# Rearranging the opening of a spectral-filter and gated-MLP kernel: doubling copies, weight loads, bank order and eviction order

## The chip, the cores and the metric

The kernel runs on one core of one Trainium2 chip. The metric is the device time of one execution in microseconds; the median of three runs before the change is 497.5 us (496.58 to 497.59). The engines are PE (matmul), DVE (vector), ACT (scalar activation), POOL (GpSimd) and SP (which only issues DMAs here). DMAs issued by POOL run on the software queue q0 and may convert fp32 to bf16 on the way; those issued by SP run on the hardware queue q1.

## The reference

```python
# x: 8 x 3072 x 256; filt_r, filt_i: 1537 x 256; w1, w2: 256 x 1024; w_out: 1024 x 256
X = np.fft.rfft(x, axis=1)
y = np.fft.irfft(X * (filt_r + 1j * filt_i), n=3072, axis=1)
t = y.reshape(8 * 3072, 256)
out = np.maximum(t @ w1, t @ w2) @ w_out
```

All inputs and the output are fp32; the kernel computes in bf16 with fp32 accumulation.

## The kernel before, in words

**The arithmetic.** A length of 3072 is split into 96 times 32. For each batch there are four matmul stages: `f1` or `s1` (a DFT of 96 with the table C1 or CT), `s2` (a DFT of 32 with twiddles, table U), a pointwise product with the filter F (`product`), `s3` (the inverse of `s2`, tables VP and VQ), and `s4` or `s4g` (the inverse of 96, table G1 or G2). The blocks v = 0 to 5 of `s2`, `product` and `s3` each cover two of twelve window groups w. The MLP then runs per tile tt of 384 tokens: max(a, b) is computed as relu(a - b) + b, so `moe_h` multiplies with Wd = w1 - w2 and takes the relu (written to gt), and `moe_o` multiplies the relu with Wo (w_out in bf16) and y with M = w2 w_out. M is made on the chip by `prep_t` (transposes of w2b, the bf16 copy of w2) and `prep_m`.

**The opening** handles batch 0 alone and keeps its intermediate values on the chip: `s1t`, `t1` (transposes into bt), `s2`, `products`, `s3t` (which writes a transposed result into zT), `t2` (transposes of zT into zr) and `s4`. `s3t` opens with one or two filler matmuls into its bank, and so does `spin` elsewhere. From the first `moe_h` on, a plan written out by hand (`plan`, `mid`, by steps of one `moe_h` each) mixes the MLP of batch b with the spectral stages of batch b + 1 and the loads of batch b + 2 (`load_xf` into three XF buffers on SP, `fold` on POOL).

**The order on each queue is the order of the program** (`manual_schedule`); engines wait for each other by semaphores, and a tile of a pool waits for the release of the buffer that it takes over. PSUM has two pools, `ps` with six banks and `pso` with two.

**What the change touches, by queue.**

- POOL's DMAs: `load_x` (L89; a chunk of x, converted to bf16, with batch 1's chunks in four transfers of 384 KB written), `load_f` (L122; the filter, sixteen transfers), `load_wo` (L294). POOL's arithmetic: `put_fz` (L142), products of blocks 0, 2, 3, 4 (L390) from copies of PSUM that `stage_x` (L652) makes on ACT, a quarter of block 5's second product (`shared_product`, L398), `prep_wd` (L298, Wd in four quarters), `cast_w2` (L291, w2b in two halves), `table_ct`.
- SP's DMAs: `load_fn` (L138), `double_f` with an engine other than DVE (L130; rows 32 to 63 and 96 to 127 of F as copies of the rows 32 below them, from SBUF to SBUF, for window groups 8 to 12), `load_w` (L287, L288; w1 and w2 in fp32 into WS, by halves of the hidden dimension), then the writes of `f1` (L338) and `load_xf` (L94).
- DVE: table arithmetic, `t1` evictions (L575), `double_f` for window groups 0 to 8 (L128, four copies), `fix_f` (L145; one row), products (L390), two evictions of `s3t` (L595).
- ACT: sines (L191 for C1, L249 for U in two halves), evictions of tables (`put_v`, L278 and L279), `stage_x` (L652), evictions of `s3t` (L597), then those of `t2` (L613), `f1` (L335), `s4` (L464) and `moe_h` (L486).
- PE: `table_v` (L265 to L269), `s2` (L384), `s3t` (L581 fillers, L587 products), `t2` (L608), `f1` (L330), `s4` (L460), `moe_h` (L482), `prep_t` (L305), `moe_o` (L536 for Wo, L534 for M), `prep_m` (L312).

At step 8 of the plan the first `moe_o` comes up, which is the first use of Wo; `prep_t` stands at steps 7 and 8, `prep_m` at step 9, and batch 1's `f1` of chunks 4 to 15 at steps 5 to 12.

Of the kernel before, what the change touches and what calls it, by code (L numbers as in the profile page):

```python
# [15 lines left out]
D = 256  # L16
HID = 1024
NP = 96
# [9 lines left out]
def kernel(  # L28
# [43 lines left out]
    setup = ExitStack()  # L72
    init = setup.enter_context(tc.tile_pool(name="init", bufs=1))
# [50 lines left out]
    def double_f(h, g, ri, engine):  # L124
        w0, w1 = WP[h]
        o_, i_ = F[64 * g + 32:64 * g + 64, ri, w0:w1], F[64 * g:64 * g + 32, ri, w0:w1]
        if engine is V:
            V.tensor_copy(o_, i_)  # L128
        else:
            nc.sync.dma_start(out=o_, in_=i_)  # L130
# [13 lines left out]
    def fix_f():  # L144
        V.tensor_copy(F[32:33, 0, 0, 0], FZ[32:33, 0])  # L145
# [10 lines left out]

    hv = init.tile([128, 2, 1], FP32)
# [22 lines left out]
    def table_c():  # L180
# [10 lines left out]
        S.activation(C1, uc.rearrange("p k r -> p (k r)"), AF.Sin, bias=zero[0:NP], scale=TWO_PI)  # L191

# [58 lines left out]
    def table_g():  # L251
        pg = ps.tile([96, NP], FP32, tag="ps", name="pg")
        TE.matmul(pg, C1, I128[0:NP, 0:NP], start=True, stop=True)
        S.activation(G1, pg, AF.Copy)
# [27 lines left out]
    WS = zrpool.tile([128, 4, HID], FP32, tag="zr", name="WS")  # L282
    w1f, w2f = WS[:, 0:2], WS[:, 2:4]

    def load_w(h):
        js = slice(512 * h, 512 * h + 512)
        nc.sync.dma_start(out=w1f[:, :, js], in_=moe_w1.rearrange("(c p) j -> p c j", p=128)[:, :, js])  # L287
        nc.sync.dma_start(out=w2f[:, :, js], in_=moe_w2.rearrange("(c p) j -> p c j", p=128)[:, :, js])  # L288

    def cast_w2(h):  # L290
        G.tensor_copy(w2b[:, :, 512 * h:512 * h + 512], w2f[:, :, 512 * h:512 * h + 512])  # L291
# [4 lines left out]
    def prep_wd(q, engine):  # L296
        js = slice(256 * q, 256 * q + 256)
        engine.tensor_tensor(Wd[:, :, js], w1f[:, :, js], w2f[:, :, js], OP.subtract)  # L298
# [23 lines left out]

    def f1(b, c, engine):
        if c == 0:
# [3 lines left out]
        at = at_[b]  # L328
        pa = ps.tile([96, 2, D], FP32, tag="ps", name="pa")
        TE.matmul(pa, C1, xb[b, c // 2][:, 2 * (c % 2):2 * (c % 2) + 2], start=True, stop=True)  # L330
# [57 lines left out]
    def product(E, v, s, px, pool=None):  # L388
# [3 lines left out]
        return pq  # L392

    def shared_product(v, s, px, xs_, pool):
        pq = pool.tile([128, 2, 2, D], BF16, tag="pq", name="pq")
        V.tensor_tensor(pq[:, 0], px, F[:, 0, 2 * v:2 * v + 2, s], OP.mult)
        V.tensor_tensor(pq[:, 1, 0], px[:, 0], F[:, 1, 2 * v, s], OP.mult)
        G.tensor_tensor(pq[:, 1, 1], xs_[:, 1], F[:, 1, 2 * v + 1, s], OP.mult)  # L398
# [178 lines left out]
    def s3t(v, pq):  # L577
        pool, tag = (ps, "ps") if v % 2 else (pso, "po")
        pz = [pool.tile([128, 2, 2, 2, 2, NM], FP32, tag=tag, name="pt%d" % g) for g in range(2)]
        for _ in range(2 if v == 1 else 1):  # L580
            TE.matmul(pz[0].rearrange("p i s r c m -> p (i s r c m)"), W1[:, 0:128], W1, start=True, stop=True)  # L581
        for i in range(2):
            for s in range(2):
                for dc in range(2):
                    for q, tab in enumerate((VP, VQ)):
                        for g in range(2):
                            TE.matmul(pz[g][:, i, s, :, dc], pq[s][64 * g:64 * g + 64, q, i, 128 * dc:128 * dc + 128],  # L587
                                      tab[64 * g:64 * g + 64, 2 * v + i, s].rearrange("p (r m) -> p r m", r=2),
                                      start=(q == 0), stop=(q == 1))
        zv = zT.rearrange("p c m (w g) q -> p w g (c m) q", g=2)  # L590
        for g in range(2):
            o_ = zv[:, 2 * v:2 * v + 2, g]
            i_ = pz[g].rearrange("p i s r c m -> p i (c m) (s r)")
            if v >= 4 and g == 1:
                V.tensor_copy(o_, i_)  # L595
            else:
                S.activation(o_, i_, AF.Copy)  # L597

    def t2(c, engines):
# [3 lines left out]
        for k, engine in enumerate(engines):  # L603
            pr = ps.tile([96, n, D], BF16, tag="ps", name="pr")
            m0 = 4 * c + n * k
            for m in range(n):
                for dc in range(2):
                    TE.transpose(pr[:, m, 128 * dc:128 * dc + 128], zT[:, dc, m0 + m].rearrange("p u q -> p (u q)"),  # L608
# [16 lines left out]
    for g in range(2):  # L625
        for ri in range(2):
            double_f(1, g, ri, nc.sync)
    for h in range(2):
        load_w(h)
# [10 lines left out]
    zT = bpool.tile([128, 2, NM, NU, 4], BF16, tag="bt", name="zT")  # L640
    for n in range(6):
        t1(n, S if n % 2 else V)
    put_v(0, 0, table_v(0, 0))
    for g in range(2):
        for ri in range(2):
            double_f(0, g, ri, V)
# [3 lines left out]
    def stage_x(v):  # L650
        t_ = init.tile([128, 2, D], FP32, name="xs%d" % v)
# [5 lines left out]
    def products(v):  # L657
        pool = pq0 if v > 2 else pqpool
        pq = [product(V, v, 0, pxs[v][0], pool)]
        if v == 5:  # L660
            pq.append(shared_product(v, 1, pxs[v][1], xs[v], pool))
        else:
            pq.append(product(G, v, 1, xs[v], pool) if v in POOLED else product(V, v, 1, pxs[v][1], pool))
# [5 lines left out]
    put_v(0, 1, table_v(0, 1))  # L669
    pxs[2] = s2(0, 2)  # L670
    stage_x(2)
    sines_u(1)
    put_v(1, 0, table_v(1, 0))
    pxs[3] = s2(0, 3)
    stage_x(3)
    put_v(1, 1, table_v(1, 1))
    for v in (1, 0, 2):
        pqs[v] = products(v)
        if v == 0:
            load_x(1, 0, 2)  # L680
    s3t(1, pqs[1])
    pxs[4] = s2(0, 4)
    stage_x(4)
    pqs[3] = products(3)
    s3t(0, pqs[0])
    pxs[5] = s2(0, 5)
    stage_x(5)
# [4 lines left out]
    for v in (4, 5):  # L692
        s3t(v, pqs[v])
    load_x(1, 2, 2)
    load_wo()
    prep_wd(0, G)
    for c in (4, 6):
        load_x(1, c, 2)
    for q in range(1, 4):
        prep_wd(q, G)  # L700
# [3 lines left out]
    setup.close()  # L704
    apool = ctx.enter_context(tc.tile_pool(name="apool", bufs=3))
# [123 lines left out]
```

## Time and profile before

| | us |
|---|---|
| median of three runs | 497.5 |
| the profiled execution | 498.64 |
| its span, first to last instruction | 496.8 |
| first transposes of `t2` start | 35.59 |
| first `moe_h` product starts | 37.73 |
| first product with Wo starts | 44.19 |

The page's busy times over the whole span are PE 483.8 us (97%), DVE 335.4 (68%), ACT 320.4 (64%) and POOL 258.7 (52%). A share over the whole span hides the opening, where PE waits and several engines take turns; so the opening is read in windows and queue by queue. All starts are us from the first instruction. In a row of a queue the first number is the start, the second the length (for several instructions, from the first to the last end), then engine, line, operation, output<-input, shapes and count; what stands in brackets is the idle time in front of it and what ended it. "Granted clock" is the share of full speed that the throttle gave PE. A DMA's time to landing counts from the start of its issue.

### The profile page before, as it was taken

The page shows a single profiled execution, that of the slowest core. Times are in us where ns is not written, and L with a number is a line of the kernel's source. Part 1 is how long each engine was busy: PE and PEld are TensorE (multiplying, and loading weights), DVE is VectorE, ACT ScalarE, POOL GpSimd, SP SyncE. Part 2 cuts the span into 40 slices and gives each one's busy share as a digit, 9 for nine tenths or more (in the row PEclk, how much of TensorE's full clock was granted, in tenths as well). Part 3 has the DMA queues.
Part 4 walks back from the last instruction along what each step waited for, and adds up shares of the span by engine and source line. Part 5 has one row for each costly group of instructions (what it writes and reads, how often), then busy time and mean ns, then how long its engine had stood idle before and what let it go on. Part 6 is the DMA issues. An engine that isn't in the chain of part 4 may idle for free.

```text
span 496.8 us, 14137 instructions
## 1 busy us (share of the span) xinstructions
PE 483.8 (97%) x5759; PEld 353.5 (71%) x5759; DVE 335.4 (68%) x535; ACT 320.4 (64%) x667; POOL 258.7 (52%) x342
## 2 busy tenths in 40 slices
PE   7699999999999999999999999999999999999997
PEld 3457777777777777777777777776777777777775
DVE  7886788468855688467855688457873688556542
ACT  5777478667775677576866668665766656464442
POOL 8694868318466594528646295536842212222220
PEclk9879999999999999999999999999999999999999
DMA  8989988996789867896789977897776834531112
GB/s 128 161 242 224 259 269 260 284 234 190 204 266 221 216 210 223 249 225 174 231 257 227 183 244 211 257 215 168 227 231 175 181 104 129 157 120 66 64 64 86
DMA packets 76626, 97.30 MB, mean 196 GB/s; under 512 B 7985, under 2 KB 54354, under 8 KB 75186
## 3 DMA queue, kind: packets, MB, share of 16 engines
q1 hardware_dynamic: 63218, 66.71, 52.1%
q0 software_dynamic: 13200, 29.60, 21.4%
q8 instruction: 45, 0.74, 0.7%
q14 instruction: 19, 0.16, 0.1%
q10 hardware_dynamic: 144, 0.09, 0.1%
HBM read 53.87 MB, written 47.19 MB: 203 GB/s over the span
## 4 chain that ended last, share of the span: by engine, by line
PE 92%; DMA 3%; ACT 2%; POOL 1%; issue 1%; DVE 0%; SPq 0%; POOLq 0%
PE po L536 34%; PE ph L482 33%; PE po L534 8%; PE pz L408 5%; PE pc L443 3%; PE px L384 2%; PE pa L355 2%; DMA xb<-in_x_dram 2%; DMA zr<-zd 1%; PE pt L587 1%; DMA zd<-zt 1%; PE pr L608 1%; POOL xb L89 1%; PE pt L581 1%; PE pa L330 1%
## 5 line engine op out<-in xcount | busy, mean ns | idle before, releaser
L486 ACT ACTIVATE gt<-ph 128x384 bf16<-128x384 f32 x357 | 175.7, 496 | 138.8 <-PE ph L482 136.2
L536 PE MATMUL po<-Wo,gt 128*128 128x256 bf16 x1528 | 262.7, 273 | 1.2 <-issue 1.2
L536 PEld LDWEIGHTS <-gt 128*128 128x128 bf16 x1528 | 144.7, 98 | 68.1 <-issue 13.5
L495 POOL DMA_DIRECT2D out_dram<-ot x186 | 103.1, 558 | 154.7 <-DVE ot L547 138.7
L390 DVE TENSOR_TENSOR pq<-px,F 128x1024 bf16<-128x1024 f32 x91 | 106.9, 1218 | 25.7 <-PE px L384 25.4
L484 DVE TENSOR_SCALAR gt<-ph 128x384 bf16<-128x384 f32 x155 | 83.6, 551 | 53.5 <-PE ph L482 47.1
L482 PEld LDWEIGHTS <-Wd 128*128 128x128 bf16 x1024 | 99.6, 98 | 13.7 <-issue 0.3
L104 POOL TENSOR_TENSOR xb<-XF 128x512 bf16<-128x512 f32 x48 | 61.3, 1277 | 66.9 <-DMA XF<-in_x_dram 31.7
L547 DVE TENSOR_SCALAR ot<-po 128x512 f32<-128x512 f32 x83 | 57.0, 686 | 35.0 <-PE po L536 33.1
L105 POOL TENSOR_TENSOR xb<-XF 128x512 bf16<-128x512 f32 x48 | 61.1, 1274 | 0.0
L359 ACT ACTIVATE at<-pa 128x512 bf16<-128x512 f32 x96 | 51.8, 611 | 3.4 <-PE pa L355 3.3
L412 ACT ACTIVATE zt<-pz 128x512 bf16<-128x512 f32 x84 | 45.6, 594 | 5.7 <-PE pz L408 1.9
L448 ACT ACTIVATE ce<-pc 128x384 f32<-128x384 f32 x56 | 23.7, 490 | 6.7 <-PE pc L443 6.0
L408 PE MATMUL pz<-pq,VP 64*64 64x256 bf16 x336 | 22.2, 281 | 0.0
L384 PE MATMUL px<-bt,U 64*64 64x256 bf16 x384 | 20.4, 283 | 1.2 <-ACT VQ L279 0.7
L408 PE MATMUL pz<-pq,VQ 64*64 64x256 bf16 x336 | 21.1, 269 | 0.0
L408 PEld LDWEIGHTS <-VP 64*64 64x64 bf16 x336 | 10.0, 105 | 13.3 <-issue 12.7
L355 PE MATMUL pa<-xb,CT 64*64 64x512 bf16 x192 | 18.0, 377 | 0.0
L443 PEld LDWEIGHTS <-zr 48*128 48x128 bf16 x896 | 13.1, 93 | 4.8 <-issue 4.4
L443 PE MATMUL pc<-G,zr 48*128 48x48 bf16 x896 | 15.4, 180 | 0.3 <-DMA zr<-zd 0.3
L384 PEld LDWEIGHTS <-U 64*64 64x64 bf16 x384 | 10.6, 109 | 3.9 <-issue 3.6
L618 PE MATMUL pd<-W 128*128 128x512 bf16 x28 | 9.2, 437 | 1.5 <-DVE zero L150 1.5
(383 smaller groups left out, 632.1 us busy)
## 6 DMA issues: line engine op xcount, KB each, us to landing
out_dram<-ot POOLq DMA_DIRECT2D x186, 128.0 KB, 3.8
XF<-in_x_dram SPq DMA_DIRECT2D x96, 192.0 KB
ad<-at SPq DMA_DIRECT2D x56, 192.0 KB
zd<-zt SPq DMA_DIRECT2D x42, 256.0 KB
zr<-zd SPq DMA_DIRECT2D x56, 192.0 KB
bt<-ad SPq DMA_DIRECT2D x13, 768.0 KB
WS<-in_moe_w_dram SPq DMA_DIRECT2D x4, 512.0 KB
xb<-in_x_dram POOLq DMA_DIRECT2D x8, 192.0 KB, 5.6
```

Source lines behind the costliest of these rows:

```text
L104: G.tensor_tensor(t_[:, 0], f[:, 0], f[:, 1], OP.add)
L105: G.tensor_tensor(t_[:, 1], f[:, 0], f[:, 1], OP.subtract)
L359: S.activation(at[:, m0:m0 + 2], pa[g], AF.Copy)
L390: E.tensor_tensor(pq, px.rearrange("p (o i) d -> p o i d", o=1).to_broadcast([128, 2, 2, D]), F[:, :, 2 * v:2 * v + 2, s], OP.mult)
L408: TE.matmul(pz[g][64 * s:64 * s + 64, i], tab[64 * g:64 * g + 64, 2 * v + i, s], pq[s][64 * g:64 * g + 64, q, i], start=(q == 0), stop=(q ...
L412: S.activation(zt[:, :, g], pz[g], AF.Copy)
L482: TE.matmul(ph, Wd[:, dc, 128 * j:128 * j + 128], y_[:, dc], start=(dc == 0), stop=(dc == 1))
L484: V.tensor_scalar(gt[tt][:, j], ph, 0.0, None, OP.max)
L486: S.activation(gt[tt][:, j], ph, AF.Relu)
L495: E.dma_start(out=dst, in_=ot[tt // 2][:, 3 * (tt % 2) + c])
L536: TE.matmul(p_, g_[:, n - 2, blk], Wo[:, n - 2], start=(e == 0), stop=(e == 9))
L547: V.tensor_scalar(ot[tt // 2][:, e - 1:e + 1], po[q // 2 % 2], SCALE, None, OP.mult)
```

## The change

The whole change lies in the opening, apart from two numbers in batch 2's load plan.

- The doubling of window groups 4 to 8 for g = 1 goes to SP's DMAs, ahead of those of groups 8 to 12; DVE keeps groups 0 to 8 for g = 0 and 0 to 4 for g = 1. `fix_f` goes to POOL.
- The first half of w1 and w2 is loaded in pieces of 256 columns (four DMAs in place of two); the second half goes into a buffer of a new pool (`whpool`), which `stage_x(3)` uses before, and is issued after `products(3)`.
- Batch 1's first x load comes after `s2(0, 4)` in place of after block 0's products; the other three and `load_wo` stand between the quarters of `prep_wd`.
- `sines_u(1)` and `table_v(1, 0)` come before `s2`; `put_v(1, 0)` follows `put_v(0, 1)`.
- Block 5's second product is done on DVE in full, with no copy by `stage_x(5)`.
- `s3t` alternates its banks over the order 1, 0, 2, 3, 4, 5; it writes PSUM with the 32 m in eights of four, zT is laid out accordingly, and the last call's eviction is cut so that its first eighth comes first. A second sine table CP holds C1's columns in the order that zT now has, for `table_g`.
- `f1` is split into its matmul (`f1_in`) and its eviction (`f1_out`); between `s3t` and the first `moe_h` four fillers (`fill`, in a `pso` bank) take the place of two `spin`s, and `f1_out` of chunks 2 and 3 moves to steps 1 and 2.
- `opool` is allocated ahead of `apool` and `zpool`. In batch 2's plan the fourth XF load moves from step 12 to 14, its fold from 20 to 23, and the next fold from 24 to 25.

```diff
-    def double_f(h, g, ri, engine):
-        w0, w1 = WP[h]
+    def double_f(w0, w1, g, ri, engine):
...
-        V.tensor_copy(F[32:33, 0, 0, 0], FZ[32:33, 0])
+        G.tensor_copy(F[32:33, 0, 0, 0], FZ[32:33, 0])
...
+        S.activation(CP.rearrange("p (g w c) -> p g w c", g=2, c=4),
+                     uc.rearrange("p (w g s) r -> p g w (s r)", g=2, s=2), AF.Sin, bias=zero[0:NP], scale=TWO_PI)
...
-        TE.matmul(pg, C1, I128[0:NP, 0:NP], start=True, stop=True)
+        TE.matmul(pg, CP, I128[0:NP, 0:NP], start=True, stop=True)
...
+    def load_w(h, cuts):
+        wh[h] = whpool.tile([128, 2, 2, 512], FP32, tag="wh", name="wh") if h else WS
+        for j0, j1 in cuts:
+            for k, w in enumerate((moe_w1, moe_w2)):
+                src = w.rearrange("(c p) j -> p c j", p=128)[:, :, 512 * h + j0:512 * h + j1]
+                nc.sync.dma_start(out=wh[h][:, k, :, j0:j1], in_=src)
...
+    def f1_in(b, c):
+        pas[c] = ps.tile([96, 2, D], FP32, tag="ps", name="pa")
+        TE.matmul(pas[c], C1, xb[b, c // 2][:, 2 * (c % 2):2 * (c % 2) + 2], start=True, stop=True)
...
     def s3t(v, pq):
-        pool, tag = (ps, "ps") if v % 2 else (pso, "po")
-        pz = [pool.tile([128, 2, 2, 2, 2, NM], FP32, tag=tag, name="pt%d" % g) for g in range(2)]
+        pool, tag = (ps, "ps") if v in (0, 3, 5) else (pso, "po")
+        pz = [pool.tile([128, 8, 2, 2, 2, 2, 4], FP32, tag=tag, name="pt%d" % g) for g in range(2)]
...
+                            TE.matmul(pz[g][:, :, i, s, :, dc].rearrange("p o r m -> p r o m"),
+                                      pq[s][64 * g:64 * g + 64, q, i, 128 * dc:128 * dc + 128],
+                                      tab[64 * g:64 * g + 64, 2 * v + i, s].rearrange("p (r o m) -> p r o m", r=2, m=4),
                                       start=(q == 0), stop=(q == 1))
...
+        for o0, o1 in ((0, 1), (1, 8)) if v == 5 else ((0, 8),):
+            for g in range(2):
+                o_ = zT[:, o0:o1, :, :, g, 2 * v:2 * v + 2].rearrange("p o c m w q -> p o (c m) (w q)")
+                i_ = pz[g][:, o0:o1].rearrange("p o i s r c m -> p o (c m) (i s r)")
...
-    for g in range(2):
-        for ri in range(2):
-            double_f(1, g, ri, nc.sync)
-    for h in range(2):
-        load_w(h)
+    for w0, w1 in ((4, 8), (8, 12)):
+        for g in range(w0 == 4, 2):
+            for ri in range(2):
+                double_f(w0, w1, g, ri, nc.sync)
+    load_w(0, ((0, 256), (256, 512)))
...
+    sines_u(1)
     for n in range(6):
         t1(n, S if n % 2 else V)
     put_v(0, 0, table_v(0, 0))
+    pv1 = table_v(1, 0)
     for g in range(2):
         for ri in range(2):
-            double_f(0, g, ri, V)
+            double_f(0, 4 if g else 8, g, ri, V)
...
-        if v == 5:
-            pq.append(shared_product(v, 1, pxs[v][1], xs[v], pool))
-        else:
-            pq.append(product(G, v, 1, xs[v], pool) if v in POOLED else product(V, v, 1, pxs[v][1], pool))
+        pq.append(product(G, v, 1, xs[v], pool) if v in POOLED else product(V, v, 1, pxs[v][1], pool))
...
     for v in (1, 0, 2):
         pqs[v] = products(v)
-        if v == 0:
-            load_x(1, 0, 2)
     s3t(1, pqs[1])
     pxs[4] = s2(0, 4)
+    load_x(1, 0, 2)
+    pqs[3] = products(3)
+    load_w(1, ((0, 512),))
     stage_x(4)
-    pqs[3] = products(3)
     s3t(0, pqs[0])
     pxs[5] = s2(0, 5)
-    stage_x(5)
...
+    prep_wd(0, G)
     load_x(1, 2, 2)
+    prep_wd(1, G)
     load_wo()
-    prep_wd(0, G)
-    for c in (4, 6):
-        load_x(1, c, 2)
-    for q in range(1, 4):
-        prep_wd(q, G)
+    prep_wd(2, G)
+    load_x(1, 4, 2)
+    prep_wd(3, G)
+    load_x(1, 6, 2)
...
-    f1(1, 0, S)
-    spin(1)
+    f1_in(1, 0)
+    fill(1)
     t2(0, (V, S))
-    f1(1, 1, V)
-    spin(1)
+    f1_in(1, 1)
+    f1_in(1, 2)
+    fill(1)
     s4(0)
-    f1(1, 2, S)
-    f1(1, 3, V)
+    f1_in(1, 3)
+    f1_out(1, 0, S)
+    f1_out(1, 1, V)
+    fill(2)
...
+    plan(0, 1, f1_out, 1, 2, S)
+    plan(0, 2, f1_out, 1, 3, V)
...
-            (8, 8, 10, 12, 17, 20, 24, 28), (10, 13, 16, 20, 24, 27, 30, 33))
+            (8, 8, 10, 14, 17, 20, 24, 28), (10, 13, 16, 23, 25, 27, 30, 33))
```

## The prediction

> **What bounds the kernel now.** I read the page first, then busy time in short windows, then the queues of PE, POOL, DVE, ACT and SP over the first 60 us, then the DMA queues and landings. In ten-microsecond windows PE is 10.00 of 10.00 from 40 us to 320 us: behind the opening nothing but PE's own work sets the time, so an edit of the opening is worth the time by which PE's unbroken stretch moves, and no more. Windows (length, busy time with count of PE, PEld, DVE, ACT, POOL, granted clock, DMA share, GB/s):
>
> ```profile
> 20.50:21.00 0.50, 0.50 (x47) 0.40 (x26) 0.47 (x2) 0.28 (x2) 0.50 (x2) 1.00 0.85 77
> 22.50:23.00 0.50, 0.00 (x0) 0.00 (x0) 0.50 (x1) 0.50 (x2) 0.00 (x0) 0.50 0.26 66
> 31.00:31.50 0.50, 0.50 (x11) 0.25 (x12) 0.50 (x1) 0.50 (x2) 0.50 (x1) 0.50 1.02 373
> 31.50:32.00 0.50, 0.50 (x31) 0.45 (x25) 0.50 (x2) 0.16 (x1) 0.50 (x1) 0.97 1.12 320
> 50.00:60.00 10.00, 10.00 (x94) 7.83 (x92) 7.06 (x13) 4.25 (x9) 8.51 (x9) 1.00 0.93 261
> ```
>
> The reader sees PE idle at 22.5, its clock at half from about 21.2 to 31.5, then full. Now the queues (start, length, instruction, idle before):
>
> ```profile
> 18.49 4.76 DVE L128 COPY F<-F 32x4096 bf16<-32x4096 bf16 x4
> 23.76 8.13 DVE L390 TENSOR_TENSOR pq<-px,F 128x1024 bf16<-128x1024 f32 x7 [0.19 <-DVE F L145]
> ...
> 26.07 6.30 POOL L390 TENSOR_TENSOR pq<-xs,F 128x1024 bf16<-128x1024 f32 x3
> 32.95 0.56 POOL L89 DMA_DIRECT2D xb<-in_x_dram  x1
> 33.51 0.93 POOL L294 DMA_DIRECT2D Wo<-in_moe_w_out_dram  x1
> 36.72 3.74 POOL L298 TENSOR_TENSOR Wd<-WS 128x512 bf16<-128x512 f32 x3
> 40.40 2.01 POOL L291 CAST w2b<-WS 128x1024 bf16<-128x1024 f32 x2
> ```
>
> ```profile
> 35.59 0.62 PE L608 MATMUL pr<-I,zT 128*96 128x128 bf16 x8 [0.34 <-DVE zT L595]
> 37.73 0.89 PE L482 MATMUL ph<-y__998,Wd 128*128 128x384 bf16 x4
> 43.74 0.61 PE L305 MATMUL pt<-I,w2b 128*128 128x128 bf16 x8
> 44.19 0.60 PE L536 MATMUL po<-Wo,gt 128*128 128x256 bf16 x4
> ```
>
> The opening ends with the transposes at 35.59; the first product with Wd runs at 37.73. Then the landing of Wo, and q0 while it moves (38 to 40 us; packets, MB, share of 16 engines):
>
> ```profile
> DMA to landing us min/median/max: 10.6/10.6/10.6
> ...
> q0 software_dynamic: 481, 0.28, 113.5%
> ```
>
> Wo is issued at 33.51 and lands at 33.51 + 10.6 = **44.11**; PE first uses it at **44.19**. That 0.08 us is the fact on which this forecast turns.
>
> **The change part by part.** All is compared with the profiled execution: 498.64 us, span 496.8 and 1.84 around it, 1.14 above the median of 497.5.
>
> *DVE.* Four copies take 4.76, 1.19 each. Of window groups 4 to 8 with g = 1 two half copies go to DMA: saved 2 x 0.6 = 1.19. The fix of one row (L145, 0.28 plus the 0.19 behind it) goes to POOL: saved 0.48. Products start at 18.49 + 3.6 = 22.1 instead of 23.76. There are now eight full ones of 8.13/7 = 1.16 (block 5's second one is no longer shared, 1.16 for 0.68 + 0.41): done at 31.4, before 32.8.
>
> *POOL.* Its filter issues end at 22.22, as before. The row fix costs between DVE's 0.28 and POOL's own cast at L142, 0.54; I take 0.5, nearer the POOL row. Then products 0, 2, the x issue (0.56, now behind product 2), products 3, 4 at 2.1 each: 22.7, 24.8, 26.9, 27.5, 29.6, 31.7; before, product 4 ended at 32.37. The shared piece (0.66) is gone. The fix waits for DVE's first copy (19.7), which is over by then. Batch 1's first x, issued at 26.9, lands 6.2 later (its landing before) at 33.1; PE's f1_in, queued ahead of the transposes, asks for it at 33.8. Then Wd quarters of 1.25 and issues in the new order: quarter 0 to 32.95, x issue to 33.5, quarter 1 to 34.75, Wo issued 34.75 to 35.7, quarter 2 to 36.95, x to 37.5, quarter 3 to 38.7, x to 39.25, casts to 40.25 and 41.25, before 41.4 and 42.4. So POOL is about 1.1 ahead, but Wo is issued 1.25 later than before.
>
> *ACT.* The extra sine of 96x96 costs 0.38 (row of L191) where ACT sits idle 1.77 at 4.3 us. The second half of U (0.93) moves from 22.97 into the 1.34 that ACT idles before 16.43. VP and VQ of the second half are then done at about 24.7, before 26.94, with one xs copy (0.60) saved. Without that idle time the sine would cost its 0.93.
>
> *PE.* The first s3t starts behind VQ's last eviction and the two products of block 1 (22.1 + 2 x 1.16 = 24.4): its two fillers at 24.8 instead of 26.0. At half clock a call is 0.54 filler + 0.97, s2 is 0.6: s3t(1) ends 26.8, s3t(0) 28.8, s3t(2) 30.9. The bank wait before s3t(2) (about 0.6, at 30.1 to 30.73, for ACT's eviction) goes, because the banks alternate. What is late next is ACT's two evictions a call, 1.09, which free s3t(4)'s bank at about 32.0; s3t(4) and (5) then end near 33.8 (before 34.7). The last eviction (0.69 on DVE) is split, so that the transposes wait for an eighth of it; a small DVE cast costs 0.28 (L145): they start at 34.15 instead of 35.59. **Gain here 1.45.** First Wd product at 36.3, first use of Wo at 42.75. The four fillers (0.22 each, before two) and the held banks lie in the time until y is evicted; without that cover 0.44.
>
> *Not shown by the trace.* Matmuls that write PSUM in runs of four: between nothing and twice the 0.57 of a call's 32, that is 0 to 3.4 over six calls; every 64-column row of L587 runs at the column rate, so I take 0. Evictions read with a stride already at L562 and L564 (0.55 and 0.43 for 384) and cost no more than contiguous ones at L484 and L486 (0.55, 0.49): 0.
>
> *SP and DMA.* Two more doubling transfers of 128 KB go ahead of the weights. Those on record took from about 20.8 (issue) to 24.6 for the first two. Their source rows land at 18.5 and 20.2, so they land at about 22.5 and 24; needed by POOL's product 2 at 24.8: hidden by 0.8. The first half of the weights goes in rows of 1 KB instead of 2 KB. From 33 to 34 us q1 moved 0.38 MB in 197 packets at 100.3%: 81 ns for 2 KB; in rows of 512 B (62 to 64 us) 1181 packets at 102.7% of 2 us: 28 ns. So 1 KB lies between 41 and 56 ns, 0 to 1.0 us for 1024 packets over 16 engines; I take 0.3. The second half waits for POOL's product 3 (29.6), whose staged input shares its buffer; nothing else is queued on SP until 36. By bytes both halves end near 34.5 to 35, as before (34.7). Batch 1's x then lands within 0.4 of before, and Wo behind it on the same queue, which is full (104 to 114% from 36 to 42): **Wo lands at 43.7, between 43.1 and 44.8**.
>
> The Trainium skill ("DMA: Bandwidth & Descriptors", Specifications) puts the smallest transfer for line rate at 512 B, by which the 1 KB rows would cost 0 and Wo land 0.3 earlier; the rows above disagree, 28 ns for 512 B being 1.4 times the per-byte time of 2 KB.
>
> *The later x load* (step 12 to 14) issues its two transfers behind batch 1's read-back; PE is 10.00 of 10 there: 0, and if that cover fails, a SP issue of 0.4.
>
> **Sum.** PE would be at Wo's first use at 42.75 but waits until 43.7, so it stands 0.45 before its old 44.19: span 496.35, execution 498.2, median **497.05**. The other 1.0 of the opening's gain turns into a wait.
>
> **Rivals.**
> *The whole gain passes.* Wo lands by 42.75: for it, the x load runs when the weights are done, and shares from 34.5 to 36 were only about 0.7; against it, Wo's own packets filled more than four microseconds at over 110%. 497.5 - 1.45 = 496.05. A clock that returns to full at 28.0 belongs here: PE is busy from 24.8 instead of idling at 25, and s3t(2), (3) at full rate would bring up to 0.4 more, 495.65. The Trainium skill ("TensorE: Matmul & The Clock Gate", Part 1) has the gate decide in free-running windows of about 3.4 us; the half-clock stretch of 10.3 us agrees, and that rule would put the earlier return at 28.
>
> *Slower: POOL becomes the bound.* Quarter 0 now stands before x and quarter 1 before Wo. If the doubled rows land late, product 2, product 3, the second half of the weights, x and Wo slip together. Between x's issue (32.95) and its first packets (about 34.3) lie 1.4 us, so Wo, issued at 34.75, could move from 36.2, while x ends at about 36.8: from 0.6 of slip on it is paid one for one. Rows 2.5 later than I have them (26.5) slip POOL 1.7: Wo at 44.8 by that, and 0.5 more where x(1,0), also late, holds PE: 45.3, **498.6**. For it: the first two such transfers took 3.8 us from issue; against it, the 0.8 in hand.
>
> *The opening does not shorten*: POOL's product 4 ends at 32.4 as before (issues end later under the added traffic), s3t(5) near 34.7, only the split helps, and Wo lands as now: 497.4.
>
> **How the numbers follow.** Forecast 0.42 (its own range 496.2 to 498.0), whole gain 0.31, POOL bound 0.18, no shortening 0.09. A measurement here tells about 0.2%, 1.0 us. Of the forecast's 0.42 some 0.12 lies beyond 1.0 faster and 0.01 beyond 1.0 slower; with the rivals: faster 0.31 + 0.12 = 0.43, slower 0.18 + 0.01 + 0.01 = 0.20, same 0.37. The range runs from the whole gain with the early clock, 495.6, to a little past the POOL case, 498.9; it leaves out the strided writes at their upper bound.
>
> **What would show it.** Right: transposes L608's counterpart near 34.2, first Wd product near 36.3, then PE idle 0.5 to 1.5 just before the first product with Wo, released by its DMA. Wrong: no idle there (whole gain), or POOL's product 2 waiting for a DMA on F, or transposes not earlier than 35.

## The result and the profile after

| | before | after |
|---|---|---|
| median, us | 497.54 | 500.82 |
| ratio, 95% interval | | 1.0064 [1.0043, 1.0084] |
| profiled execution, its span, us | 498.64, 496.8 | 501.47, 499.7 |
| first transposes of `t2` start | 35.59 | 33.87 |
| first product with Wd starts | 37.73 | 36.09 |
| first product with Wo starts | 44.19 | 48.77 |

One of the changed kernel's six executions took 1249.35 us; the median contains it and the ratio doesn't. By the ratio the change makes the kernel 3.2 us slower; the forecast was 497.05, 0.45 faster. Measured once more on another chip, beside other runs, the ratio was 1.0047 [1.0035, 1.0059].

The queue of PE after the change (start, length, instruction, idle time in front and its releaser):

```profile
33.87 0.62 PE L615 MATMUL pr<-I,zT 128*96 128x128 bf16 x8
...
36.09 0.86 PE L488 MATMUL ph<-y__1003,Wd 128*128 128x384 bf16 x4
...
41.14 0.82 PE L488 MATMUL ph<-y__1003,Wd 128*128 128x384 bf16 x2 [3.09 <-POOL Wd L303]
...
48.77 0.60 PE L542 MATMUL po<-Wo,gt 128*128 128x256 bf16 x4
```

The opening arrives 1.64 us earlier at the first product with Wd, and the third quarter of Wd isn't there. The same stretch in windows, first of the kernel after, then of the kernel before (length, busy time of PE, PEld, DVE, ACT and POOL with counts, granted clock, DMA share, GB/s):

```profile
36.09:38.05 1.96, 1.96 (x17) 1.15 (x15) 1.81 (x4) 1.37 (x3) 1.42 (x2) 1.00 1.09 231
38.05:41.14 3.09, 0.01 (x1) 0.00 (x1) 1.16 (x3) 0.49 (x1) 1.31 (x2) 0.90 0.90 156
41.14:48.77 7.63, 7.63 (x54) 5.38 (x55) 3.83 (x7) 4.06 (x7) 4.89 (x8) 0.59 1.10 207
```

```profile
37.73:44.19 6.46, 6.46 (x72) 4.75 (x71) 5.94 (x12) 5.22 (x10) 5.35 (x8) 1.00 1.15 201
```

PE does the same work in both: 1.96 + 7.63 x 0.59 = 6.46 us of full clock, as before. So the 4.58 us by which the first product with Wo is later divide as: 1.64 gained, **3.09 of wait for Wd, and 3.13 because the clock was at half from the end of that wait on** (from 40.5 to 47.4; 7.63 us for 4.50 us of work). The span grows by 2.9 only. Of the 1.68 between, 1.27 is idle time of PE behind 50 us, of which this execution has less than the one before:

```profile
50.00:490.00 440.00, 439.77 (x5068) 325.57 (x5066) 296.42 (x454) 285.12 (x596) 220.49 (x282) 1.00 0.74 199
```

```profile
50.00:490.00 440.00, 438.50 (x5058) 324.55 (x5056) 295.65 (x452) 284.28 (x595) 221.40 (x282) 1.00 0.73 198
```

The first line is after, the second before: 0.23 us of idle PE against 1.50 (the largest piece before: 1.23 at 336.35, for which the profile shows no releaser). This idle time differs between executions, of one kernel too: it is 0.70 in a second profile of the changed kernel, and over all the profiles below it lies between 0 (`e14_half_before`) and 3.20 (`e6_both_order`). So one profile tells what the opening does, and the executions of a run together tell the time.

Why Wd is late is on POOL and SP after the change:

```profile
33.59 1.27 POOL L303 TENSOR_TENSOR Wd<-WS 128x512 bf16<-128x512 f32 x1 [1.79 <-DMA WS<-in_moe_w_dram]
34.80 0.56 POOL L90 DMA_DIRECT2D xb<-in_x_dram  x1
35.37 1.28 POOL L303 TENSOR_TENSOR Wd<-WS 128x512 bf16<-128x512 f32 x1
36.59 0.92 POOL L299 DMA_DIRECT2D Wo<-in_moe_w_out_dram  x1
39.83 1.26 POOL L303 TENSOR_TENSOR Wd<-wh 128x512 bf16<-128x512 f32 x1 [2.32 <-DMA wh<-in_moe_w_dram]
```

```profile
18.71 7.27 SPq L130 DMA_DIRECT2D F<-F  x6
26.03 3.62 SPq L293 DMA_DIRECT2D WS<-in_moe_w_dram  x4
29.76 1.46 SPq L293 DMA_DIRECT2D wh<-in_moe_w_dram  x2
```

and in the chain of waits that ended last (start, length, what):

```profile
21.10 4.32 DMA F<-in_filt_i_dram
25.42 0.02 SPq L130
...
29.76 0.42 SPq L293
30.18 0.04 issue
30.22 9.53 DMA wh<-in_moe_w_dram
39.75 0.07 issue
39.83 1.27 POOL Wd L303
41.10 0.05 issue
41.14 0.82 PE ph L488 x2
```

Two things are to be seen. POOL waits twice for weights, 1.79 and 2.32 us; x and Wo stand behind the first wait, and Wo is issued at 36.59 (33.51 before). And the second half of the weights, issued at 29.76, needs 9.53 us and lands at 39.75. What it shares the DMA engines with is seen in the queues from 29 to 30 us (packets, MB, share of 16 engines), after and then before:

```profile
q0 software_dynamic: 34, 0.14, 83.6%
q1 hardware_dynamic: 8, 0.01, 2.1%
```

```profile
q0 software_dynamic: 38, 0.16, 78.3%
q1 hardware_dynamic: 34, 0.07, 19.8%
```

While batch 1's x, issued at 27.01 on POOL's queue, moves, the weights on SP's queue all but stop (0.01 MB in each of the two microseconds 29 to 31; before, beside the same x, 0.07 and 0.16). The stretch from 25 to 30 us shows the sum of it, after and then before:

```profile
25.00:30.00 5.00, 4.05 (x118) 2.67 (x121) 3.83 (x4) 2.95 (x7) 4.99 (x4) 0.81 0.69 145
```

```profile
25.00:30.00 5.00, 4.79 (x127) 2.75 (x126) 5.00 (x5) 3.33 (x8) 4.99 (x4) 0.50 0.75 204
```

145 GB/s against 204 over 5 us is 0.3 MB that the changed kernel still has to move when the DMA engines are full (share 1.02 from 30 to 35).

### The profile page after: what moved, and what is told of

It reads as the page before. It is cut to its first block, busy times and chain, and to the rows that moved or that the text cites. A ratio compares the mean times of both kernels' runs of the same rounds, so it can differ in the third digit from the quotient of the medians.

```text
span 499.7 us, 14150 instructions
## 1 busy us (share of the span) xinstructions
PE 485.5 (97%) x5757; PEld 355.3 (71%) x5761; DVE 334.5 (67%) x534; ACT 320.8 (64%) x668; POOL 257.4 (52%) x342
## 4 chain that ended last, share of the span: by engine, by line
PE 91%; DMA 4%; POOL 2%; SPq 1%; issue 1%; DVE 0%; POOLq 0%
PE po L542 35%; PE ph L488 33%; PE po L540 8%; PE pz L414 5%; PE pc L449 3%; PE pa L368 2%; PE px L397 2%; DMA wh<-in_moe_w_dram 2%; DMA xb<-in_x_dram 2%; POOL F L123 1%; DMA F<-in_filt_i_dram 1%; SPq L293 1%; POOL xb L90 1%; PE pa L336 1%; PE pr L615 1%
## 5 line engine op out<-in xcount | busy, mean ns | idle before, releaser
L403 DVE TENSOR_TENSOR pq<-px,F 128x1024 bf16<-128x1024 f32 x92 | 108.1, 1218 | 26.8 <-PE px L397 25.4
```

What stands on the lines that cost most here:

```text
L403: E.tensor_tensor(pq, px.rearrange("p (o i) d -> p o i d", o=1).to_broadcast([128, 2, 2, D]), F[:, :, 2 * v:2 * v + 2, s], OP.mult)
```

## The experiments

**Theory:** the gain of the opening is real and is lost to landings of weights, x and Wo, because these were made later, or no earlier, while PE needs them earlier. **Rivals:** batch 2's plan, the additional doubling transfers, POOL's order or the 1 KB rows by itself. Each group of runs has its own runs of the kernel before on its chip (medians 497.6 to 498.2); a difference between groups counts for less than one within a group. All ratios are against the kernel before.

### One part of the change undone

`e1_early`: all weights issued together; block 3's staged input gets a buffer of its own, so that the second half need not wait for it.

```diff
     load_w(0, ((0, 256), (256, 512)))
+    load_w(1, ((0, 512),))
...
     pqs[3] = products(3)
-    load_w(1, ((0, 512),))
```

> The changed kernel, but the second half of w1 and w2 is issued on SP right behind the first (two transfers of 512 KB), into a buffer that block 3's staged input no longer shares. Theory L (the second half comes late because its issue waits for POOL's product 3 at 29.7 and then shares the engines with x): it lands before 36.5, POOL does not wait for it, PE's 3.1 us wait for Wd and the half clock behind it are gone, PE reaches the first product with Wo at about 43 to 44.5 instead of 48.8, and the time is 496.0 to 497.5. Rival R (the rows of 1 KB in the first half let x take the engines, so that both halves come late): the second half still lands after 38, PE still waits 1.5 us or more for Wd, and the time stays at 499 to 501.

Measured 1.0031 [1.0014, 1.0049]. PE in its trace, from the third quarter on:

```profile
39.67 0.50 PE L488 MATMUL ph<-y__1003,Wd 128*128 128x384 bf16 x2 [1.76 <-POOL Wd L303]
...
41.13 0.42 PE L336 MATMUL pa<-xb,C 96*96 96x512 bf16 x1 [0.29 <-DMA xb<-in_x_dram]
...
42.99 0.62 PE L310 MATMUL pt<-I,w2b 128*128 128x128 bf16 x8 [0.48 <-POOL w2b L296]
...
45.55 0.60 PE L542 MATMUL po<-Wo,gt 128*128 128x256 bf16 x4
```

The wait for Wd is 1.76 instead of 3.09, the clock stays full, and the first product with Wo is at 45.55 instead of 48.77. In its place stand a wait for x and one for w2b, whose casts come last on POOL, behind its own waits for weights (1.39 and 1.23): the wait removed uncovers the next. The second half landed just after 38 (quarter 2 starts at 38.36), and with the wait and the time (499.39) that is what rival R expected, not theory L: the late issue isn't the cost by itself.

`e2_halves`: the first half in rows of 2 KB, the second half still late. `e3_both`: the old loading, both halves in rows of 2 KB, issued together (the diff is that of `e2_halves`; `e3_both` has the one of `e1_early` as well).

```diff
-    load_w(0, ((0, 256), (256, 512)))
+    load_w(0, ((0, 512),))
```

> The changed kernel, but the first half of w1 and w2 in two transfers of 512 KB with rows of 2 KB, in place of four with rows of 1 KB; the second half is as changed, behind product 3. Theory L: the issue of the second half stays at 29.7 and its landing moves by less than 1.5 us from 39.75; PE still waits 2 us or more for Wd, time 499 to 501. Rival R: the first half is through before x takes the engines, the second lands before 37, PE waits less than 1 us, time below 498.

> The changed kernel with the old weight loading: four transfers of 512 KB, rows of 2 KB, one behind the other, no shared buffer. Both theories: no wait for Wd. By the prediction's own forecast (Wo lands at 43.7 whatever the opening gains) PE waits at the first product with Wo until about 43.7 and the time is 496.5 to 497.5; if the opening's gain passes whole, the first product with Wo runs at 42.6 and the time is 495.7 to 496.3.

Measured 1.0037 [1.0014, 1.0061] and 1.0035 [1.0017, 1.0053]. `e2_halves` is about as theory L had it (waits of 1.80 and 0.42 for Wd). `e3_both` misses what both theories expected, no wait for Wd: PE waits 0.41, 0.52 and 1.41 us for it and 0.65 for x, and the first product with Wo is at 46.21. With whole rows quarter 0 starts at 34.62 in both (33.59 in the changed kernel, 33.21 in `e1_early`): the pieces do bring the first quarter 1.0 to 1.4 us earlier. On the time `e1_early` and `e3_both`, on one chip, do not differ (499.39 and 499.5), so the row size, rival R's cause, is no cost that shows here.

`e5_order`: POOL's old order, the rest as changed. `e6_both_order`: the same with the old weight loading.

```diff
-    prep_wd(0, G)
     load_x(1, 2, 2)
-    prep_wd(1, G)
     load_wo()
-    prep_wd(2, G)
-    load_x(1, 4, 2)
-    prep_wd(3, G)
-    load_x(1, 6, 2)
+    prep_wd(0, G)
+    for c in (4, 6):
+        load_x(1, c, 2)
+    for q in range(1, 4):
+        prep_wd(q, G)
```

> The changed kernel with POOL's old order behind the products: x, Wo, Wd's quarter 0, two x, quarters 1 to 3. Theory O (POOL waits for the first half of the weights ahead of the x and Wo issues, and these and the casts come late): Wo is issued near 32.5 instead of 36.6 and no longer stands behind a wait, but the second half of the weights, issued at 29.7, now shares the engines with x and Wo, lands after 40, and PE waits for Wd until 41 to 43: time 499.5 to 502. If the order were all there is to it, the first product with Wo comes before 45 and the time is below 498.

> The changed kernel with the old weight loading (as the third experiment) and with POOL's old order too. Theory O: Wo is issued near 32.5 and lands at 43 to 44.5, the first product with Wo comes at 43 to 44.8, time 496.3 to 497.7; that would be the forecast's own case, the gain of the opening turned into a wait for Wo. Rival D (the doubling transfers and the later first x load make the weights late whatever the order is): PE waits 1 us or more for Wd, the first product with Wo comes at 45.5 or later, time 498.5 to 500.

Measured 1.0073 [1.0047, 1.01] and 1.0045 [1.0028, 1.0061]. In `e5_order` Wo is issued at 31.98, but PE waits 3.97 us for the third quarter (41.34 on POOL, which waits 4.88 for the weights): x and Wo now move ahead of them. So POOL's new order alone is not the cost. In `e6_both_order` PE waits 1.02 for Wd and the first product with Wo is at 44.35, as before the change and as theory O had it; the time (500.29) is not. The profiled execution idles 3.2 us behind 50 us, 1.22 of it waiting for a read-back of zr at 100.06; whether the other executions lose their time there too isn't known.

`e9_plan_back`: batch 2's old load plan.

```diff
-            (8, 8, 10, 14, 17, 20, 24, 28), (10, 13, 16, 23, 25, 27, 30, 33))
+            (8, 8, 10, 12, 17, 20, 24, 28), (10, 13, 16, 20, 24, 27, 30, 33))
```

> The changed kernel with batch 2's old load plan (fourth XF load at step 12, folds at 20 and 24). Theory P (the later load keeps SP busy until 73 in place of 65, so batch 1's zd writes, its zr reads and batch 2's bt read come late, which PE meets only if it is early): here PE is 4.6 us late at the first product with Wo anyway, so the move back gains at most 0.7: 499.8 to 501.5. If the plan were the larger part of the loss, the time falls below 499.3.

Measured 1.0021 [1.0001, 1.0042], lower than the changed kernel, on another chip, and at 499.59 just under what was expected. Its trace still has the waits for Wd (1.44 and 0.41) and a first product with Wo at 46.72; nothing behind 60 us accounts for a gain by the plan. `e11_plan_alone` and `e18_early_plan` below bear on it.

### One part of the change alone, on the kernel before

`e4_gate` and `e8_gate_alone` put the late second half into the kernel before, the latter with `opool` allocated first (the last line of the diff), `e7_order_alone` POOL's new order (the diff of `e5_order` reversed), `e11_plan_alone` the new plan (the diff of `e9_plan_back` reversed).

```diff
-    for h in range(2):
-        load_w(h)
+    load_w(0)
...
     pqs[3] = products(3)
+    load_w(1)
...
+    opool = ctx.enter_context(tc.tile_pool(name="opool", bufs=2))
```

> The kernel before, with one part of the change alone: the second half of w1 and w2 goes into a buffer that block 3's staged input uses first, and is issued behind block 3's products (two transfers of 512 KB); the first half stays in two transfers with rows of 2 KB. Theory L: the issue moves from 26.3 to about 30.3, the half lands at 37.5 to 40, POOL waits for it before Wd's third quarter, PE waits 0.5 to 3 us, and the time is 498 to 501. Rival R: with rows of 2 KB the second half lands before 37 and the time stays within 0.5 us of before.

> The kernel before with POOL's new order alone (quarter 0, x, quarter 1, Wo, quarter 2, x, quarter 3, x). Theory O: quarter 0 waits for its weights until 33.5 to 34.5, x is issued near 35.3 instead of 33.0 and Wo near 37 instead of 33.5, Wo lands at 45 to 47 and PE waits for it (or for x of chunk 4) 1 to 3 us: time +1 to +3 over before. If the order is free, because the queue is full anyway, as the prediction had it: within 0.5 of before.

> The kernel before with the late second half alone (as the fourth experiment), and with the output pool allocated ahead of the pool of f1's evictions, so that no eviction waits for the weights' buffer. Theory L: the second half lands at 37.5 to 40, Wd's third quarter and with it the third of the first tile's products waits up to 2 us: time +0.5 to +2.5 over before. Rival O (the late half is harmless while x and Wo are issued early): within 0.5 of before.

> The kernel before with the new load plan of batch 2 alone. Theory P: SP's loads of XF behind batch 1's bt read hold the first zd write until 71 to 74 instead of 66.4, PE waits for zr or bt 0.5 to 3 us in all between 95 and 170, time 0.7 to 3 us over before. If the plan is free: within 0.4 of before.

Measured: `e4_gate` 1.017 [1.0145, 1.0194], `e8_gate_alone` 1.0006 [0.9988, 1.0024], `e7_order_alone` 1.0015 [0.9994, 1.0035], `e11_plan_alone` 0.9996 [0.998, 1.0011]. `e4_gate` measures something else: the weights' new buffer lies where eviction buffers come later, and ACT's evictions wait for it (PE waits 7.37 us at 45.56). It shows why the change moves `opool` to the front, which `e8_gate_alone` does too. There the second half is issued at 30.43, yet the third quarter does not wait, and the first product with Wo is at 44.50: theory L missed again. In `e7_order_alone` Wo is issued at 36.67, and PE waits 0.30 for it and 0.70 for x, the least that theory O expected; the time doesn't show it. None of the three parts costs the kernel before anything that shows in the time. That each costs something under an opening that needs the data earlier isn't shown.

### The opening alone

`e10_opening_only` is the changed kernel with the old weight loading, POOL order and plan together; `e12_x_early` also issues batch 1's first x where it was:

```diff
     for v in (1, 0, 2):
         pqs[v] = products(v)
+        if v == 0:
+            load_x(1, 0, 2)
     s3t(1, pqs[1])
     pxs[4] = s2(0, 4)
-    load_x(1, 0, 2)
```

> The changed kernel with three parts undone: the old weight loading, POOL's old order and batch 2's old load plan (the sixth experiment with the old plan). Theory P: the first zd write is issued near 66 again instead of 73, PE's waits for zr and bt near 100 and 115 are gone, and the time falls from 500.3 to 496.8 to 498.0. If the plan is free, it stays at 499.8 to 500.8.

> The tenth experiment with batch 1's first x back behind block 0's products. Theory X (the later x load stops the weights for 2 to 3 us while it runs, 27 to 30, and comes late for f1): PE's waits for x near 34 (0.4) and for Wd's third quarter near 39.6 (1.0) shrink by 0.5 or more in sum, the first product with Wo comes at 43.3 to 44.2, time 0.2 to 1.0 below the tenth. If x's place is free: within 0.3 of the tenth.

Measured 1.0022 [0.9994, 1.0051] and 1.0007 [0.9989, 1.0026]: no gain in either, and no loss that shows. DVE in the profiled execution of `e12_x_early`, at 501.26 one of its slowest (the median is 498.77), shows what an early x can do:

```profile
31.98 1.23 DVE L403 TENSOR_TENSOR pq<-px,F 128x1024 bf16<-128x1024 f32 x1 [3.81 <-DMA F<-F]
```

With x issued at 25.04 the doubled rows of groups 8 to 12, now behind two more transfers, come 3.81 us late for block 4's product; from 26 to 29 us SP's queue moves nothing. In the changed kernel x goes 2 us later, DVE waits 1.17 for the same rows, and the weights pay. The doubling, x and the weights want the same three microseconds. That this is why the typical execution gains nothing is argued, not shown.

`e15_double_dve` takes the two transfers back to DVE; `e16_double_dve_early` does so on top of `e1_early`.

```diff
-    for w0, w1 in ((4, 8), (8, 12)):
-        for g in range(w0 == 4, 2):
-            for ri in range(2):
-                double_f(w0, w1, g, ri, nc.sync)
+    for g in range(2):
+        for ri in range(2):
+            double_f(8, 12, g, ri, nc.sync)
...
-            double_f(0, 4 if g else 8, g, ri, V)
+            double_f(0, 8, g, ri, V)
```

> The changed kernel with the doubling as before: four transfers on SP for window groups 8 to 12, all of groups 0 to 8 by DVE. Theory (late second half of the weights and POOL's order are the cost): first half of the weights is issued 1 us earlier (25.0) and quarter 0 waits less (under 1.0 us, 1.79 with six transfers), products start 1.2 later, the second half still waits for product 3 and lands near 39 to 40: PE waits 2 to 3 for Wd's third quarter, ratio 1.004 to 1.007. Rival (the doubling by DMA ahead of the weights is the cost): ratio 1.002 or less, wait for Wd under 1.

> The run before it with the second half of the weights issued right behind the first as well (own buffer), so that all weights are issued about 25.0 to 29, as in the kernel before. Theory: the weights land as before (bulk by 35.5), third quarter waits under 0.5, what is left is POOL's order (Wo issued near 36, lands near 44.8): ratio 1.000 to 1.002, under the 1.003 of the same run with six transfers. Rival (the doubling by DMA costs nothing, the weights would be as late without it): ratio 1.003 or more, quarter 0 waits 1.4 as with six transfers.

Measured 1.005 [1.003, 1.007] and 1.0035 [1.0017, 1.0053]. The first has the time and the wait that the theory expected (PE waits 2.79 for Wd in the profiled execution, at 504.14 its slowest; the median is 500.52), although the weights were issued no earlier there (27.30). The second misses it and has the rival's time: no wait for Wd is left, but the transposes start only at 36.96, DVE's four copies having ended at 24.5, and the first product with Wo at 46.07. So the two transfers are not the cost by themselves. How much of the opening's gain hangs on them isn't settled: without them the transposes start at 36.96 in the second and at 34.75 in the first (35.59 before the change).

### The weights' bytes taken away

`e13_half_old_order` is `e5_order` without the load of the second half; what is worked out from it takes the first half's data, with the same instructions. `e14_half_before` does so to the kernel before.

```diff
-        wh[h] = whpool.tile([128, 2, 2, 512], FP32, tag="wh", name="wh") if h else WS
+        wh[h] = WS
...
-    load_w(1, ((0, 512),))
+    wh[1] = WS
```

> The changed kernel with only the first half of the MoE weights loaded (the second half of the difference Wd and of w2 is worked out from the first half's data; 1 MB less moves in the opening) and POOL's old order of x, Wo and quarters. Theory (the opening's gain is real and is lost only to landings of weights, x and Wo): no wait for Wd above 0.3 us, first product with Wo between 42.4 and 43.4 us (it was 44.19 before and 48.77 in the changed kernel), clock full behind 40, median 0.8 to 1.5 us under the kernel before (ratio 0.997 to 0.9985). Rival (the gain is lost elsewhere: batch 2's plan, the read-backs of zr and bt, the clock): first Wo as early, yet the ratio is 1.000 or more, with idle time of PE behind 60 us.

> The control: the kernel before with only the first half of the weights loaded, its quarters worked out from that half. Theory: it never waited for weights, so the lack of 1 MB moves only Wo and x, which landed at their use: first Wo 43.8 to 44.2, ratio 0.999 to 1.0005. Rival (the relief of the DMA engines itself is worth the time, whichever opening stands ahead of it): ratio 0.998 or less, as much as the run with the changed opening gains.

Measured 0.9982 [0.9964, 1.0001] and 1.0001 [0.9985, 1.0017]. Against `e5_order` (1.0073) one thing differs, the load of 1 MB, and it is worth 0.9% (on different chips); the first product with Wo is at 45.27 where it was at 48.89. The kernel before gains nothing from the same relief. This is the run that carries the theory: **the changed opening is slower because of the second half of the weights, and that half costs only the changed opening.** Leaving it out takes away its bytes and the waits for its landing together; the two aren't told apart. The trace is less neat than expected:

```profile
35.33 0.62 PE L615 MATMUL pr<-I,zT 128*96 128x128 bf16 x8
...
39.31 0.82 PE L488 MATMUL ph<-y__1000,Wd 128*128 128x384 bf16 x4 [0.44 <-POOL Wd L303]
...
40.53 0.50 PE L488 MATMUL ph<-y__1000,Wd 128*128 128x384 bf16 x2 [0.39 <-POOL Wd L303]
...
45.27 0.60 PE L542 MATMUL po<-Wo,gt 128*128 128x256 bf16 x4
```

In this execution the doubling occupied SP until 27.0, the opening was 1.5 us later than in the other trace, and even the first half alone came late; for the first product with Wo 42.4 to 43.4 was expected. What the second half costs is read from the twelve executions against those of `e5_order`. That the opening is faster than before without it isn't shown: the interval just includes 1 and overlaps that of `e14_half_before`, on the same chip.

### The remaining question: the plan

`e17_after_again` is the changed kernel once more; `e18_early_plan`, on the same chip, is `e1_early` with `e9_plan_back`.

> The changed kernel itself once more, beside the next run on the same chip, since the runs so far stand on different chips and the distance of the changed kernel from the run with batch 2's old plan (0.4%) is larger than any idle time behind 60 us shows. Theory (the loss is in the opening, 3 us): ratio 1.004 to 1.008, first product with Wo between 46.5 and 49 us. Rival (the first measurement was high): ratio 1.002 to 1.004.

> The changed kernel with the second half of the weights issued right behind the first and batch 2's old load plan, POOL's new order and six doubling transfers kept. Theory (only the opening counts, the plan is worth nothing): as the run with the early second half alone, ratio 1.002 to 1.0045. Rival (the plan costs 0.2 to 0.4% of its own): ratio 0.999 to 1.001.

Measured 1.0047 [1.0035, 1.0059] and 1.0047 [1.0035, 1.0059]: both edits together gain nothing on this chip. With `e11_plan_alone` that speaks against the plan, as the theory had it, but the earlier weights show no gain here either, slightly over what was expected. The profiled execution of `e17_after_again` waits 1.40 and 0.26 us for Wd and 0.47 for w2b with the clock full, and its first product with Wo is at 46.37: the loss in the opening is 2.2 to 4.6 us, by execution. In `e18_early_plan` PE has no wait for Wd at all, and the chain of waits says what took its place:

```profile
26.39 6.77 DMA WS<-in_moe_w_dram
33.15 0.02 issue
33.18 0.02 POOLq L303
33.20 0.09 issue
33.29 1.21 POOL Wd L303
34.50 7.02 DMA xb<-in_x_dram
41.52 0.04 issue
41.56 0.42 PE pa L336
```

```profile
41.56 0.42 PE L336 MATMUL pa<-xb,C 96*96 96x512 bf16 x1 [1.71 <-DMA xb<-in_x_dram]
```

POOL waits for the first half of the weights, only then issues x, x needs 7.02 us, and PE waits 1.71 for x instead of Wd. This is the part that POOL's new order plays in this execution: x behind a wait for weights.

No version ran faster than the kernel before in a way the runs can tell; the one that leaves 1 MB out comes nearest to it.

## Why the prediction was wrong

**Right:** that PE is all but unbroken behind the opening (439.77 of 440 us busy; 436.80 in `e6_both_order`), that the opening would gain about 1.45 (transposes 33.87 for a forecast 34.15, first product with Wd 36.09 for 36.3), that the gain could turn into a wait for data, ACT's times (second VQ half done at 24.5, forecast 24.7), nothing for strided PSUM writes (a row of `s3t` takes 0.20 as before) and nothing for batch 2's plan (0.9996 alone). The clock came back to full at 26.9 instead of 31.5, as the first rival had it (it put it at 28.0).

**Partly luck.** The path to the transposes was not the forecast's. DVE's products ended at 32.86, where the forecast had 31.4 and the kernel before 32.81: a wait of 1.17 for doubled rows took most of what DVE had saved. The earlier full clock, which the forecast left to a rival, worked the other way, and the two misses offset each other; no run separates them.

**Its signs.** The idle time of 0.5 to 1.5 us in front of the first product with Wo didn't come: PE runs into it without a wait. (The sum's 0.45 is 0.49 by its own 44.19 and 43.7; nothing hangs on it.)

**The step that failed** is in "SP and DMA": "By bytes both halves end near 34.5 to 35, as before (34.7)". The first half landed at 33.5 and the second at 39.75. Three terms were missing from it:
- Issue. The weights are issued at 26.03 (25.07 before), the first half in four issues of 3.62 us in all. The chain above shows what holds SP's queue: the last doubling transfer (L130) waits for the filter's last piece, which lands at 25.42. SP waits 2.0 us for such pieces, 0.7 before. The number of doubling transfers isn't it: with four instead of six the weights were issued at 27.30 (`e15_double_dve`) and 26.89 (`e16_double_dve_early`). Why the piece landed later isn't shown.
- Company. In the kernel before q1 moved 0.07 to 0.34 MB a microsecond from 27 to 32, with batch 1's x beside it from 28 on; the forecast took the weights to land as there. Beside the same x they now get 0.01 a microsecond from 29 to 31, and beside the next x, from 37 to 39, the second half's tail gets 0.04 and 0.05.
- Order. The second half is issued at 29.76, last of all; POOL's wait of 2.32 us for it holds quarter 2, and behind it x, quarter 3 and x. A late issue alone need not cost that: in `e8_gate_alone` it comes at 30.43, and POOL doesn't wait.

**What hung on it.** POOL's row without waits (quarter 0 at 31.7, Wo issued at 34.75) became 33.59 and 36.59, and Wo landed near 45.4 for a forecast 43.1 to 44.8. That no longer mattered: PE asked for the third quarter of Wd at 38.05, 3.09 us ahead of it. The forecast looked for the wait at Wo because Wo was the one landing on the edge (44.11 for 44.19); it gave no due time to Wd's quarters, which before had been ready at every use.

**Doubled rows.** "Hidden by 0.8" held here for POOL's product 2, which did not wait, but not in `e1_early` (0.56) and `e18_early_plan` (0.80). The rows of groups 8 to 12, two places further back in the queue, were not in the sum: DVE waits 1.17 for them at 28.2. The row fix on POOL took 0.70 for 0.5.

**The rivals.** "POOL becomes the bound" was nearest in kind: it names quarter 0 ahead of x and quarter 1 ahead of Wo. It tied this to late doubled rows instead of late weights, and its 498.6 has no term for the clock. A wait of 3.09 us cost 3.13 more by the half clock that went with it; where the clock stayed full (`e17_after_again`) the loss was 2.2 at the first product with Wo. The range ended at 498.9 because the weights had no late bound at all.

**Open.** How the loss divides between the late issue, x beside the weights and POOL's order isn't settled: undoing the late issue gave 1.6 us against the first measurement of the changed kernel (1.0064 to 1.0031, on different chips and with overlapping intervals) and, with the old plan, nothing on the chip of `e17_after_again`; what it removes comes back as the next wait. Why `e6_both_order` is slow with an opening no later than before is open too. Why x stopped q1 less in the kernel before isn't shown either.

## What to carry to other kernels

If a stage is to start earlier, write down for every transfer it consumes when it must land now, when it is issued now, and what runs on the other queue at that time; a transfer that had slack before is not safe because it landed in time before. A wait in the opening is priced with the clock behind it. And where undoing one part moves a wait instead of removing it, leave the suspected bytes out of both kernels: that pair told here what the single edits didn't, though not whether the bytes or the wait for them is the cost.

## What the hardware showed that was not expected

**One queue starves the other.** With x on q0 moving 0.14 to 0.18 MB in a microsecond (34 to 50 packets, 84 to 104% of the engines' time), q1 with weights issued and waiting moved 7 or 8 packets, 2 to 3%. In `e17_after_again` it moved none from 29 to 30 us and 2 from 30 to 31. The Trainium skill ("DMA: Bandwidth & Descriptors", Queues, rings and completion order) has each engine take turns between queues, packet by packet. The kernel before agrees from 29 to 30 us (38 packets and 34); the changed kernel, with 34 and 8, does not, if the page's packets are those that the profile counts, which isn't shown.

**Short gaps halve the clock, sometimes.** A wait of PE, for Wd or in `e18_early_plan` for x, was followed by half clock for 3.4 us in `e9_plan_back` (1.44 us of wait; half from 41.8 to 45.2), `e2_halves` (1.80; 41.9 to 45.3), `e18_early_plan` (1.71; 42.5 to 45.9), `e15_double_dve` (2.79; 41.7 to 45.1) and `e5_order` (3.97; 42.6 to 46.0), and for 6.8 us in the changed kernel (3.09; 40.5 to 47.4), worked out from the granted clock in windows of 0.5 us; behind 1.40 in `e17_after_again`, 1.41 in `e3_both` and 1.76 in `e1_early` the clock stayed full. The Trainium skill ("TensorE: Matmul & The Clock Gate", Part 1) has the gate decide in free-running windows of about 3.4 us; the lengths, one window and two, agree with it. By its wording the fall takes an idle window; here three waits of about half a window were enough, and three were not.

**The opening differs between executions of one kernel.** The changed kernel started its transposes at 33.87 in one profile and at 34.91 in another, and its first product with Wo at 48.77 and 46.37.
